# Retention and SwiGLU in one kernel: one step per chunk, subtractions of weight units on GpSimd, and a new layout of the first down stage

## The chip, the cores and the metric

The kernel runs on one core of a Trainium2 chip. The metric is the device time of one execution in microseconds (us), as a median over several runs. Engine names: PE is TensorE, DVE is VectorE, ACT is ScalarE, POOL is GpSimd, and SP is SyncE, whose queue issues most of the DMAs. Each engine takes its instructions strictly in the order of its own queue. Lines such as L707 are those of the kernel before.

## The reference, cut to what matters

```python
# q, k, v: (4, 8, 768, 64), float32; gamma and scale are constants of a head
for t in range(S):
    state = gamma * state + einsum('bhd,bhe->bhde', k[:, :, t], v[:, :, t])
    y[:, :, t] = scale * einsum('bhd,bhde->bhe', q[:, :, t], state)
x = y.transpose(0, 2, 1, 3).reshape(3072, 512)
g = x @ w_gate                        # 512 x 1536
h = g / (1 + exp(-g)) * (x @ w_val)   # w_val: 512 x 1536
return h @ w_out                      # 1536 x 512
```

## The kernel before, in words

The retention is computed in chunks of 128 time steps. For each chunk there are four pieces of work. `scores` multiplies k and q on PE (16 small matmuls, L385) and applies a decay mask on DVE (two operations, L391). `mix` forms the chunk's output y on PE from the old state (16 matmuls, L442; a sequence's first chunk has none) and from the masked scores (16 matmuls, L446), and ACT copies it to `xT` (L449). `state` brings the state up to date on PE (16 matmuls, L424) and DVE (L429), after ACT has decayed the old one (`decay`, four operations, L411). `scale_q` and `scale_k` scale operands on POOL (L399, L404).

The 3072 rows are worked on in four segments `s` of 2 x 384 rows (3 chunks of two sequences each). Each segment has an up stage (both of the first two weight matrices and the gate) and a down stage (the product with `w_out`). Both use a block scheme with seven products in place of eight, so sums and differences of blocks of the weights ("T" or "U" blocks) and of the activations are needed beforehand. The first segment's up stage is `up` (L513). The other three use `up2`, which applies the scheme a second time.

**The second up stages (`up2`).** They walk over 21 weight units `n`. A unit lies in one of six slots of `ring` and has seven products `U11, U1, U2, U22, U3, U21, U4`, of four matmuls each (L624), at the places `7n, 7n+2, ..., 7n+12` of an order that is sorted by these numbers, so that neighbouring units interleave. The products are added up in PSUM, and between them PSUM is read by ACT copies or DVE additions (both L589). For most units POOL adds two of these copies to older sums ("the diagonal", place `7n+2.6`, L589). A DVE addition at place `7n+8.5` needs that diagonal, and product `U4` at `7n+12` adds into the bank that this addition reads. POOL also forms sums for `hT` (L659), in two blocks, for two units of each seven. A whole unit (896 KB) is read back from DRAM (`unitt`) if its sums were formed earlier. Otherwise a 512 KB half (`unitb`) is read, three subtractions complete it (`sums_u`: one of 512 elements, L170, and two of 256, L178 and L174, in every partition), and a DMA of SP writes it to `unitt` for the later segments. A load of unit n+6 is issued at place `7n+13.2`.

**The down stages (`down`).** For each of three row blocks `u` there are seven products of 12 matmuls (L707, L716): `first` (into a bank that is copied), T1, T2, B22, T3, `second` and T4. The bank `x` is read by a DVE addition after T3 (L772) before T4 may add into it. After every product `step()` is called, 21 times in a stage, and carries a count `k`. In the first three down stages `step()` also hands out the retention of the next segment (the list `steps`), and in the down stage of segment 0 the loads and the subtractions of units 5, 7, ..., 19 and 0 to 3 as well (12 units, on DVE). What is left of the lists runs after the last product. Also in segment 0, the sums of the T blocks of `w_out` (`sums_d`, L289) and the states of the last two chunks of the first segment (`do("t4")`, `do("t5")`) lie between the first products. Activation sums for a row block are formed on DVE (`sum_h`, L695), and those for the next up stage by `sums_x` (L496 to L499) and `sums_2` (L578 to L581). After T4 ACT copies the last quarter (L778) and issues two DMAs to the output (L782).

In the first down stage no `second` stands between T3 and T4 for u = 0 and 1; in the others one does.

Of the kernel before, what the change touches and what calls it, by code (L numbers as in the profile page):

```python
# [16 lines left out]
P = 128  # L17
# [7 lines left out]
L = 3  # L25
# [8 lines left out]
RING = 6  # L34
# [7 lines left out]
def tile_retnet_swiglu(  # L42
# [79 lines left out]
    def seg_chunks(s):  # L122

        p, pos = divmod(s * L, NCK)
        return [(2 * p + i) * NCK + pos + j for j in range(L) for i in range(2)]
# [327 lines left out]
    def retention(s):  # L453

        cs = seg_chunks(s)

        def first(n):
            scores(cs[n])  # L460
            scale_k(cs[n])
            scale_q(cs[n])

        def last(n):
            decay(cs[n])
            state(cs[n])
            del chunks[cs[n]]
            if n + 3 < len(cs):
                load_chunk(cs[n + 3], places_of(n))

        steps = [lambda: first(0)]
        for n, c in enumerate(cs):
            if n + 1 < len(cs):
                steps.append(lambda n=n: first(n + 1))
            steps.append(lambda c=c: mix(c))
            steps.append(lambda n=n: last(n))
            if n % 2:
                steps.append(lambda n=n: sums_x(n // 2))
        return steps

# [102 lines left out]
    def up2(s, prepared, at_end):  # L583
# [4 lines left out]
        def at(t, fn, *args, **kw):  # L588
            events.append((t, len(events), lambda: fn(*args, **kw)))  # L589
# [17 lines left out]
        def stage(n):  # L607
# [61 lines left out]
                at(base + 13.2, load_unit, n + RING, n + RING in prepared)  # L669
            m = n + 2  # L670
            if m < NU and m not in prepared:
                for when, k in ((2.2, 0), (4.8, 1), (6.8, 2)):
                    at(base + when, lambda k=k: sums_u(m)[k]())

        for n in range(NU):
            stage(n)
# [23 lines left out]
    def down(s, u, step):  # L700
# [38 lines left out]
        if u == 0:  # L739
            first(0, range(2, FH))  # L740
            first(1)
            if s == 0:

                sums_d(0)
                sum_h(1, 0)
                second(0)
                do("t4")
                sum_h(2, 0)
                sums_d(1)
                second(1)  # L750
                do("t5")
                sum_h(4, 0)
                sum_h(3, 0)
                sums_d(2)
        elif u == 2:
            first(u)
        cur = dict(hs)
        wb = bank("wz")[:, :DH]
# [15 lines left out]
        step()  # L774
        if s or u == 2:
            second(u)
        product(x, T4, a_dn(1, 1, u), start=False)
        nc.scalar.copy(ev[1][:, :DH], x)  # L778
        p, pos = divmod(s * L, NCK)
        for i in range(2):  # L780
            row = (2 * p + i) * S + (pos + u) * P
            nc.scalar.dma_start(out=out[ds(row, P)], in_=ev[i])  # L782
        step()


    kept_vk = consts.tile([P, 2, 512], F32, name="kept_vk")
# [42 lines left out]
        g4 s5 S0 g5 x1 m4 a1 q5 C0 U T0 b1 m5 x2 U D D  # L829
    """)  # L830

    def retain(k):
        for _ in range(k):
            if steps:
                steps.pop(0)()

    for f in range(NF - 1):
        up(f)
# [9 lines left out]

    resident = list(range(RING - 2))
    to_sum = list(range(RING - 1, NU, 2)) + resident
    prepared = set(to_sum)

    for s in range(NSEG):
        nxt = seg_chunks(s + 1) if s + 1 < NSEG else []
        if s == 0:
            for i in range(3):
                load_chunk(nxt[i], places_of(i))
        else:  # L860

            ends = [(7 * n + 13.4, lambda i=i: load_chunk(nxt[i], places_of(i)))
                    for i, n in ((0, NU - 5), (2, NU - 4), (1, NU - 3)) if nxt]


            def begin(s=s):
                down(s, None, None)(0, range(2))

            ends.append((7 * (NU - 1) + 11, begin))
            for n in range(RING - 2, RING):  # L870
                ends.append((-1, lambda n=n: load_unit(n, n in prepared)))
            up2(s, prepared, ends)
            prepared = set(range(NU))
        if s:
            for n in (1, 2, 4, 3):
                sum_h(n, 0)
        steps = []
        if nxt:
            att.clear()
            steps = retention(s + 1) + [lambda ps=ps: sums_2(*ps)  # L880
                                        for ps in ((5, 6), (1, 2), (7,))]
        count, sums = [0, 0, 0], []

        def step():

            k = count[0] = count[0] + 1
            retain((k > 2) + (4 < k < 13) if s else (k > 5) + (7 < k < 18))
            if not nxt:
                return
            if s:  # L890
                if k > 7 and k % 2 == 0 and k // 2 - 4 < RING - 2:
                    load_unit(k // 2 - 4, True)
                return
            if count[1] < len(to_sum) and count[1] * 15 < (k - 5) * len(to_sum):
                n = to_sum[count[1]]
                load_unit(n, False, n if n in resident else count[1] % (RING - 2))
                sums.extend(sums_u(n))
                count[1] += 1
            while sums and count[2] * 15 < (k - 6) * 3 * len(to_sum):
                sums.pop(0)()  # L900
                count[2] += 1

        for u in range(L):
            down(s, u, step)
        for st in steps + sums:
            st()
        if nxt:
            sums_2(3)
            sums_2(4)

# [48 lines left out]
```

## Time and profile before

| | |
|---|---|
| median of 4 runs | 734.3 us (733.88 to 735.89) |
| profiled execution | 738.21 us, of which the span of the trace is 736.4 us |
| PE busy | 715.9 us (97% of the span) |
| DVE, ACT, POOL busy | 468.9, 239.6, 237.2 us |
| first up stage, to 146.7 us | first segment |
| first down stage, to 230.24 us | holds the retention of segment 1 and 12 units' subtractions |
| up2 of segment 1, from 230.24 to 331.78 us | 101.54 us |
| down of segment 1, to 407.77 us | 75.99 us |
| up2 of segment 2, to 505.28 us | 97.51 us |
| down of segment 2, to 581.96 us | 76.68 us |
| up2 of segment 3, to 679.14 us | 97.18 us |
| last down stage, to the end | no retention beside it |

How to read it: times count from the span's start, and a stage begins here with the start of its first matmul (the four to eight matmuls of the next stage that are drawn ahead are not counted apart). PE is "busy" from the start of a matmul to its modelled end, so matmuls that follow each other closely overlap and a busy PE may still run below its best pace; what a matmul really takes of the path is the distance from its start to the next one's start.

### The profile page before, as it was taken

How to read it: one execution, taken by the hardware profiler on the slowest of the kernel's cores; microseconds unless marked ns; L12 is line 12 of the kernel's file. 1: busy time of each engine (PE TensorE's matmuls, PEld its weight loads, DVE VectorE, ACT ScalarE, POOL GpSimd, SP SyncE). 2: the span in 40 equal slices, each digit the busy share in tenths (PEclk: the TensorE clock that was granted, in tenths of full speed). 3: DMA queues.
4: the chain of work that ended last, by engine and by line, in shares of the span. 5: the costliest groups of instructions: out<-in, count | busy, mean ns of one | idle time of the engine just before them, and what ended most of it. 6: DMA issues, size and time to landing. Idle time of an engine off the chain costs nothing.

```text
span 736.4 us, 11713 instructions
## 1 busy us (share of the span) xinstructions
PE 715.9 (97%) x4544; PEld 618.0 (84%) x4544; DVE 468.9 (64%) x836; ACT 239.6 (33%) x484; POOL 237.2 (32%) x147
## 2 busy tenths in 40 slices
PE   7998999999999999999999999999999999999997
PEld 6754555577878999998888999998888999999886
DVE  3687998777668788886454465757526356667420
ACT  2558777511122333321121324332121133233000
POOL 0423444503200638280310174464210063726000
PEclk9899999999999999999999999999999999999999
DMA  8698887703998867671643355560283055540010
GB/s 309 211 350 277 273 289 255 278 1 104 406 347 308 298 219 265 236 240 33 210 162 126 128 201 201 200 215 20 87 301 131 28 200 201 200 150 1 1 57 29
DMA packets 60824, 139.06 MB, mean 189 GB/s; under 512 B 4576, under 2 KB 27616, under 8 KB 60768
## 3 DMA queue, kind: packets, MB, share of 16 engines
q1 hardware_dynamic: 57312, 132.01, 51.7%
q10 hardware_dynamic: 3456, 6.29, 2.3%
q8 instruction: 36, 0.59, 0.3%
q14 instruction: 20, 0.16, 0.1%
HBM read 101.72 MB, written 36.57 MB: 188 GB/s over the span
## 4 chain that ended last, share of the span: by engine, by line
PE 87%; DVE 4%; issue 1%; ACT 1%; DMA 1%; ACTq 0%; SPq 0%; DVEq 0%
PE bank L624 38%; PE bank L707 23%; PE bank L513 14%; PE bank L716 4%; PE bank L385 3%; PE bank L446 2%; PE bank L442 2%; PE bank L424 1%; DMA ring<-unitb 1%; DVE iop L589 0%; DVE ring L289 0%; DVE ring L170 0%; DVE midp L391 0%; ACT midp L589 0%; DVE hsp L695 0%
## 5 line engine op out<-in xcount | busy, mean ns | idle before, releaser
L624 PE MATMUL bank<-loadp,ring 128*128 128x192 f32 x720 | 140.7, 327 | 3.1 <-ACT midp L589 2.5
L707 PE MATMUL bank<-wot,hsp 128*128 128x256 f32 x576 | 131.7, 383 | 0.0
L624 PEld LDWEIGHTS bank<-loadp,ring 128*128 128x128 f32 x720 | 120.5, 190 | 4.8 <-ACT midp L589 3.6
L707 PEld LDWEIGHTS bank<-wot,hsp 128*128 128x128 f32 x576 | 107.5, 190 | 16.6 <-issue 1.0
L589 DVE TENSOR_TENSOR iop<-bank,iop 128x384 f32<-128x384 f32 x144 | 79.7, 555 | 56.2 <-PE bank L624 53.2
L624 PE MATMUL bank<-xs,ring 128*128 128x192 f32 x432 | 87.9, 326 | 0.0
L659 POOL TENSOR_TENSOR hT<-iop 128x768 f32<-128x768 f32 x36 | 66.4, 1845 | 36.8 <-DVE iop L589 36.8
L589 ACT COPY hsp<-bank 128x384 f32<-128x384 f32 x90 | 42.8, 478 | 100.5 <-PE bank L624 89.8
L589 POOL TENSOR_TENSOR iop<-hsp,midp 128x768 f32<-128x768 f32 x9 | 16.3, 1813 | 181.6 <-ACT hsp L589 181.6
L624 PEld LDWEIGHTS bank<-xs,ring 128*128 128x128 f32 x432 | 73.2, 190 | 0.0
L707 PE MATMUL bank<-wot,hT 128*128 128x256 f32 x288 | 66.2, 383 | 2.5 <-DVE iop L772 2.5
L513 PE MATMUL bank<-xs,ring 128*128 128x384 f32 x192 | 64.7, 488 | 3.2 <-DVE xs L496 1.8
L624 PE MATMUL bank<-xT,ring 128*128 128x192 f32 x324 | 66.2, 327 | 1.1 <-DVE iop L589 1.1
L707 PEld LDWEIGHTS bank<-wot,hT 128*128 128x128 f32 x288 | 53.8, 190 | 10.8 <-DVE iop L772 2.8
L513 PEld LDWEIGHTS bank<-xs,ring 128*128 128x128 f32 x192 | 36.1, 190 | 30.0 <-issue 2.4
L624 PE MATMUL bank<-hsp,ring 128*128 128x192 f32 x288 | 56.8, 327 | 0.0
L624 PEld LDWEIGHTS bank<-xT,ring 128*128 128x128 f32 x324 | 54.8, 190 | 2.3 <-DVE iop L589 2.2
L589 DVE TENSOR_TENSOR midp<-bank,midp 128x384 f32<-128x384 f32 x72 | 40.0, 555 | 22.8 <-PE bank L624 21.2
L513 PE MATMUL bank<-xT,ring 128*128 128x384 f32 x144 | 49.3, 488 | 1.6 <-DVE hT L550 1.6
L624 PEld LDWEIGHTS bank<-hsp,ring 128*128 128x128 f32 x288 | 48.4, 190 | 0.5 <-ACT hsp L589 0.5
L449 ACT COPY xT<-bank 128x512 f32<-128x512 f32 x24 | 14.1, 586 | 95.1 <-PE bank L446 95.0
L513 PEld LDWEIGHTS bank<-xT,ring 128*128 128x128 f32 x144 | 27.1, 190 | 21.0 <-DVE hT L550 2.2
(146 smaller groups left out, 971.0 us busy)
## 6 DMA issues: line engine op xcount, KB each, us to landing
ring<-unitt SPq DMA_DIRECT2D x50, 896.0 KB, 4.6
unitt<-ring SPq DMA_DIRECT2D x21, 896.0 KB, 4.7
unitb<-ring SPq DMA_DIRECT2D x12, 896.0 KB, 7.4
ring<-unitb SPq DMA_DIRECT2D x21, 512.0 KB, 6.5
out_dram<-iop ACTq DMA_DIRECT2D x24, 256.0 KB, 3.5
loadp<-in_w_val_dram SPq DMA_DIRECT2D x18, 256.0 KB, 3.9
loadp<-in_w_gate_dram SPq DMA_DIRECT2D x9, 512.0 KB, 6.6
midp<-in_w_out_dram SPq DMA_DIRECT2D x12, 256.0 KB, 6.3
```

Source lines behind the costliest of these rows:

```text
L385: nc.tensor.matmul(sp[i][:, ts(n, P)], kt[r, n], qt[r, n], start=True, stop=True, skip_group_check=True)
L424: nc.tensor.matmul(st[ds(D * i, D), n], kd[:, h], vn[:, h], start=(n == 0), stop=True, skip_group_check=True)
L442: nc.tensor.matmul(y[r, ts(n, P)], prev[r, n], qd[r, n], start=(n == 0), stop=False, skip_group_check=True)
L446: nc.tensor.matmul(y[ds(D * i, D), ts(n, P)], vn[:, ts(2 * n + i, D)], a[i][:, n], start=(ci == 0 and n == 0), stop=True, skip_group_check ...
L449: nc.scalar.copy(xT[:, :, c // NCK % 2, ts(ci % L, P)], pairs(y))
L513: nc.tensor.matmul(o, w[:, slot, k], a[:, k], start=(start and k == 0), stop=(stop and k == KH - 1), skip_group_check=True)
L589: events.append((t, len(events), lambda: fn(*args, **kw)))
L624: nc.tensor.matmul(o[:, h], w[:, h, slot], rhs, start=(start and h == 0), stop=True, skip_group_check=True)
L659: by_block(9.5, 13.5, lambda r: pool(to[:, r], u2[:, r], p5[:, r], op=add))
L707: nc.tensor.matmul(o, a[:, k], wot[k][:, slot], start=(start and k == 0), stop=(k == FH - 1), skip_group_check=True)
L716: nc.tensor.matmul(o, a_dn(0, 0, u)[:, k], wot[k][:, B11], start=(k == 0), stop=(k == FH - 1), skip_group_check=True)
```

## The change

Five edits, all in the order of the work; no arithmetic is added or left out.

1. `retention` makes one step of each chunk: scores of chunk n+1, then mix, decay and state of chunk n and the load of chunk n+3, then the two scalings of chunk n+1. Before, these were three steps, with products of the down stage between them. The steps are handed out at fixed counts, `DUE`, where before `retain` took one or two at a time.
2. `sums_2(1, 2)` moves to right after the last chunk's step, `sums_2(5, 6)` is the last step, and `sums_2(7)` runs after the last product.
3. In the first down stage the states of both last chunks are put together, and for u = 0 and 1 a product stands between T3 and T4: `second(1)` and `first(2)`, which were elsewhere in the same stage.
4. In the first three down stages the last row block's output DMAs are issued at place 5 of the following up2 and not at the end of the down stage.
5. The first down stage prepares 10 units (5, 7, ..., 19, 0, 1) and no longer 12. It loads units 2 and 3 too, but their three subtractions, as those of 4, 6, ..., 20, are done by POOL in the up2 of segment 1 (11 units there; before 9, on DVE), at places 4.1 to 4.3 and not 2.2 to 6.8. Loads of units begin after the second product of the first down stage, three ahead of the subtractions.

```diff
 def retention(s):
-        def first(n):
-            scores(cs[n])
-            scale_k(cs[n])
-            scale_q(cs[n])
-        def last(n):
-            decay(cs[n])
-            state(cs[n])
-            del chunks[cs[n]]
-            if n + 3 < len(cs):
-                load_chunk(cs[n + 3], places_of(n))
-        steps = [lambda: first(0)]
-        for n, c in enumerate(cs):
+        def chunk(n):
             if n + 1 < len(cs):
-                steps.append(lambda n=n: first(n + 1))
-            steps.append(lambda c=c: mix(c))
-            steps.append(lambda n=n: last(n))
-            if n % 2:
+                scores(cs[n + 1])
+            if n >= 0:
+                mix(cs[n])
+                decay(cs[n])
+                state(cs[n])
+                del chunks[cs[n]]
+                if n + 3 < len(cs):
+                    load_chunk(cs[n + 3], places_of(n))
+            if n + 1 < len(cs):
+                scale_k(cs[n + 1])
+                scale_q(cs[n + 1])
+        steps = []
+        for n in range(-1, len(cs)):
+            steps.append(lambda n=n: chunk(n))
+            if n == 5:
+                steps.append(lambda: sums_2(1, 2))
+            if n > 0 and n % 2:
                 steps.append(lambda n=n: sums_x(n // 2))
...
 # up2, stage n
-                for when, k in ((2.2, 0), (4.8, 1), (6.8, 2)):
-                    at(base + when, lambda k=k: sums_u(m)[k]())
+                for when, k in ((4.1, 0), (4.2, 1), (4.3, 2)):
+                    at(base + when, lambda k=k: sums_u(m, nc.gpsimd)[k]())
...
 # down, u == 0 and s == 0
-                do("t4")
+                do("t4 t5")
                 sum_h(2, 0)
                 sums_d(1)
-                second(1)
-                do("t5")
...
-        elif u == 2:
+        elif u == 2 and s:
             first(u)
...
         if s or u == 2:
             second(u)
+        else:
+            (second, first)[u](u + 1)
         product(x, T4, a_dn(1, 1, u), start=False)
         nc.scalar.copy(ev[1][:, :DH], x)
-        for i in range(2):
-            row = (2 * p + i) * S + (pos + u) * P
-            nc.scalar.dma_start(out=out[ds(row, P)], in_=ev[i])
+        def store():
+            for i in range(2):
+                row = (2 * p + i) * S + (pos + u) * P
+                nc.scalar.dma_start(out=out[ds(row, P)], in_=ev[i])
+        if u < L - 1 or s == NSEG - 1:
+            store()
         step()
+        return store
...
+    DUE = [(5, 7, 9, 10, 11, 13, 14, 15, 17, 18, 19, 20),
+           (3, 5, 7, 8, 9, 11, 12, 13, 15, 16, 18, 20)]
...
-    resident = list(range(RING - 2))
+    resident = [0, 1]
...
+            ends.append((5, store))
             up2(s, prepared, ends)
...
-            steps = retention(s + 1) + [lambda ps=ps: sums_2(*ps)
-                                        for ps in ((5, 6), (1, 2), (7,))]
+            steps = retention(s + 1) + [lambda: sums_2(5, 6)]
 def step():
-            retain((k > 2) + (4 < k < 13) if s else (k > 5) + (7 < k < 18))
...
             if s:
+                if k in DUE[1]:
+                    steps.pop(0)()
...
-            if count[1] < len(to_sum) and count[1] * 15 < (k - 5) * len(to_sum):
-                n = to_sum[count[1]]
-                load_unit(n, False, n if n in resident else count[1] % (RING - 2))
-                sums.extend(sums_u(n))
+            if count[1] < len(to_sum) + 1 and k > 1 and count[1] < 3 + count[2] // 3:
+                n = (to_sum + [2])[count[1]]
+                load_unit(n, False, count[1] % (RING - 2))
+                if n in prepared:
+                    sums.extend(sums_u(n))
                 count[1] += 1
-            while sums and count[2] * 15 < (k - 6) * 3 * len(to_sum):
+            if k in DUE[0]:
+                steps.pop(0)()
+            while sums and count[2] * 12.5 < (k - 6) * 3 * len(to_sum):
...
         for u in range(L):
-            down(s, u, step)
-        for st in steps + sums:
+            store = down(s, u, step)
+        for st in sums:
             st()
+        if s == 0:
+            load_unit(3, False)
         if nxt:
+            sums_2(7)
             sums_2(3)
             sums_2(4)
```

## The prediction

> **What bounds the kernel.** I read the page first.
>
> ```profile
> PE 715.9 (97%) x4544; PEld 618.0 (84%) x4544; DVE 468.9 (64%) x836; ACT 239.6 (33%) x484; POOL 237.2 (32%) x147
> PE 87%; DVE 4%; issue 1%; ACT 1%; DMA 1%; ACTq 0%; SPq 0%; DVEq 0%
> ```
>
> PE is the bound, busy 97% of the span and 87% of the chain that ended last. The change takes no matmul away, so a gain can only come from matmuls that start closer together. Next, the chain in order of time (start, length, what), in the down stage of segment 2 and in the last one, which has no retention:
>
> ```profile
> 513.44 2.79 PE bank L707 x12
> 516.23 1.09 PE bank L385 x16
> 517.32 2.79 PE bank L707 x12
> 520.11 1.02 PE bank L442 x16
> 521.13 1.02 PE bank L446 x16
> 522.15 0.46 PE bank L424 x16
> ...
> 531.33 0.62 PE bank L424 x16
> ...
> 683.46 31.08 PE bank L707 x144
> ```
>
> Undisturbed, a product of 12 takes 31.08/12 = 2.59 us. Between small matmuls it takes 2.79. So each interruption costs 0.20 us beyond its own matmuls. A state (L424) right behind its own mix takes 0.46, alone 0.62.
>
> Then who made PE wait (us in total, times, longest):
>
> ```profile
> PE bank L707 <- DVE iop L772: 2.5, 2, 1.8
> PE bank L624 <- ACT midp L589: 2.5, 4, 1.3
> PE bank L624 <- DVE iop L589: 1.8, 3, 0.7
> ```
>
> The timeline gives their places. Since a matmul's end is modelled, I measure a stall from start to start:
>
> ```profile
> 175.37 0.63 PE L424 MATMUL bank<-loadp 128*64 128x64 f32 x16
> 177.77 0.92 PE L707 MATMUL bank<-wot,hT 128*128 128x256 f32 x3 [1.77 <-DVE iop L772]
> ...
> 230.89 0.81 PE L624 MATMUL bank<-loadp,ring 128*128 128x192 f32 x4
> 232.45 1.57 PE L624 MATMUL bank<-loadp,ring 128*128 128x192 f32 x8 [0.75 <-ACT midp L589]
> ```
>
> The first pair is T4 in the first down stage, which waits for a DVE read (2.40 us from start to start, 0.56 without the wait). The second is the start of an up2 (1.56, where four matmuls take 0.65). Last, the three up2 stages side by side (length, then busy time of PE, PEld, DVE, ACT, POOL, clock, DMA share, GB/s). The first is 4.0 us longer and its DVE has 22 us more to do:
>
> ```profile
> 230.24:331.78 101.54, 98.08 (x594) 96.01 (x592) 81.58 (x142) 33.84 (x66) 54.10 (x30) 1.00 0.73 262
> 407.77:505.28 97.51, 96.95 (x594) 96.20 (x592) 59.47 (x104) 34.12 (x66) 49.48 (x28) 1.00 0.52 180
> ```
>
> **The change part by part.**
>
> **One step per chunk.** In the timelines of the three down stages with retention I count 13, 12 and 11 places where small matmuls stand between products. In the order of the changed program there are 8, 7 and 7 (seven steps, and t4 with t5). That is 14 fewer at 0.20: 2.8 us. Seven states stood apart from their mix (2, 3 and 2) and now follow it, at 0.62 - 0.46 = 0.16: 1.1 us. Together 3.9 us, on the path. The new waits inside a step have cover. Mix n needs masks and scaled q of scores n, which ran a chunk step earlier. Between the two chunk steps lie two products (5.4 us), the rest of that step (2.5) and scores n+1 (1.1), 9 us against 1.4 for two masks (0.68 each) and 2.4 for the POOL scalings (1.31 and 1.11). On DVE the state addition now waits about 1.2 us for matmuls with the rest of the queue behind it; DVE is busy 61.9 of the 85.2 us from 146.7 to 231.92, so up to 6 us of that fit. I take 0; without the cover each of 20 steps could hold PE, and at 0.1 us each that is 2 us.
>
> **A product between T3 and T4.** The two stalls on L772 are 2.40 - 0.56 = 1.84 and (202.25 to 203.64) 1.39 - 0.56 = 0.83, together 2.7 us. The read was late because DVE was behind by activation sums slowed beside POOL (1.90 and 1.68 us for the pair where one alone is 0.95), masks and unit subtractions. Now 2.6 us of a product lie between, which covers both. What is late next is T4 of u = 2, where sums_2(1, 2) (4 x 0.55) and two subtractions stand before L772 in DVE's queue: 0.42 + 2.2 + 0.9 + 0.4 = 3.9 us after B22 ends, against two products, 5.2. It holds by 1.3. First use of the T blocks comes 2.8 us earlier, since `second(1)` left its place: sums_d(1) would end at about 160.3 (its row ends there now), and T2 would start at 160.0 and need its last block 2.2 us later. It holds.
>
> **The late output DMAs.** They stood in ACT's queue before the first copy of up2. PE lost 1.56 - 0.65 = 0.91 us there, and at 408.91 and 583.09 0.36 each, 1.6 in all. At place 5 they stand between copies at 4.5 and 7.5, two products (1.3 us) apart, and an issue takes 0.34 to 1.16. They read space that up2 first writes at place 16.6, near 10 us; issued at 3.2 us with a landing of 2.1 to 8.3, they are most often done. I take a gain of 1.6, and 0 to 0.7 lost.
>
> **Subtractions on POOL.** Removed are two PE stalls in the first up2, both behind subtractions: 0.85 at 243.4 (a 512 subtraction that ran 1.81) and 1.48 at 264.8 (L174 ahead of L663, for which an ACT copy waited). 2.3 us.
>
> What POOL pays the trace shows only by neighbours: 1.27 for 512 elements (L399) and 1.81 for 768, so 0.73 for 256 on that line, and 2.73 for a unit. Two multiples bound a 256: 0.64 from below, 1.27 from above (as long as a 512), so 2.6 to 3.8 a unit. I take 2.73, from the nearest shapes. 11 units are 30 us on 49, 79 of 97. The stage has room, its middle less. These rows are from the second up2, where POOL runs as it will there:
>
> ```profile
> 453.99 1.81 POOL L659 TENSOR_TENSOR hT<-iop 128x768 f32<-128x768 f32 x1 [2.13 <-DVE iop L589]
> ...
> 463.09 1.81 POOL L659 TENSOR_TENSOR hT<-iop 128x768 f32<-128x768 f32 x1 [1.84 <-DVE iop L589]
> 464.86 1.81 POOL L589 TENSOR_TENSOR hT<-hsp,hT 128x768 f32<-128x768 f32 x1
> 466.63 1.82 POOL L659 TENSOR_TENSOR hT<-iop 128x768 f32<-128x768 f32 x1
> 468.53 1.81 POOL L589 TENSOR_TENSOR iop<-hsp,iop 128x768 f32<-128x768 f32 x1
> ```
>
> In this seven (units 7 to 13) unit 12's subtractions fall before the row at 463.09, whose 1.84 us of idle time swallow all but 0.9; unit 14's stand before 466.63 and add 2.73. So unit 13's diagonal (468.53) ends not at 470.34 but at 474.0, and its DVE addition at 474.6. U4 of unit 13 is due after 100 products of 0.65 from 407.77 + 0.36, at 473.3: PE waits 1.3 us. The same for units 0 to 6 and 14 to 20 gives 0.1 each. I add 0.6 where L663 meets a POOL operation (0.95 alone, 1.3 to 1.8 beside one), and 0.5 at the start, where subtractions of units 2 and 3 on POOL meet sums_2(3) and (4). New waits: 2.6 us, net loss 0.3. Bounds: no new wait (a gain of 2.3) and every POOL operation 20% slower, as rows of 2.19 beside DVE's own subtractions show (a loss near 13, the last rival). SP's queue: the store of unit n+2 now stands before the load of unit n+5 and holds it until POOL is done, at most 4 us late; that unit is used 18 us later, and loads landed in 6.8 (9.7 at worst). 0.
>
> The Trainium skill, GPSIMD Engine Reference, section 4.1, speaks against this edit: it gives elementwise work on a tile to VectorE, as GpSimd is about half as fast on two inputs. Its figure, 4497 ns for 2048 elements, would make a unit about 2.2 us of stream time, an estimate, and the wait at unit 13 some 0.9 shorter. The rows here agree on the ratio (0.69 on DVE, 1.27 on POOL) but not on the verdict, since in this stage DVE is the engine that PE waits for.
>
> Two units fewer take 3.9 us from DVE in the first down stage, off the path. Loads begin earlier there, in a stretch (150 to 175) where DMA stood near 0. 0.
>
> **Sum.** 3.9 + 2.7 + 1.6 - 0.3 = 7.9 us less. The profiled execution, 738.2, would become 730.3, its span 728.5. It lies 3.9 above the median of 734.3; the same difference on the median gives 726.4.
>
> **Rivals.**
> - All cover holds and POOL never delays PE: 3.9 + 2.7 + 1.6 + 2.3 = 10.5, so 723.8. For it: POOL idles half of the stage. Against: the 0.9 us at unit 13 that are missing by the bare count. Chance 0.2.
> - DVE stays behind in the first down stage, since each step's state addition now blocks it, and the stalls at T4 come back at another product, or the steps cost 0.1 to 0.2 each: the 2.7 goes and 1 more with it, 730.1. For it: DVE has 9.80 of 10 us from 170 to 180. Chance 0.14.
> - No change: the counted interruptions cost nothing when merged, because PE meets new waits of their size. The order of the changed program shows fewer places, so the edit does what it says, and only waits could undo it. 734. Chance 0.03.
> - Slower: POOL becomes the bound of the first up2. If its 768 operations take 2.19 and a unit 3.3, the middle seven have 9 x 2.19 + 2 x 3.3 = 26.3 us between two diagonals that PE passes in 22.8. That is 3.5 too many, and with DVE and the next load waiting behind I take 5 for each of three sevens, 15 in all. 10.5 - 15 gives 4.5 us more, 738.8. It decides once a unit costs POOL over 4 us: the waits 0.1, 1.3 and 0.1 grow by two units a seven, and 1.5 + 6 x (4.05 - 2.73) = 9.4 eats what the edits leave (10.5 less 0.6 and 0.5). Against: the rows of 2.19 stood beside DVE's subtractions, which are gone; without them they are 1.81. Chance 0.08.
>
> My forecast has 0.55, from 724.5 to 728.5. The range takes in the first rival and the second with 1.4 us for the unknown costs: 722.8 to 731.5. A measurement of this kernel can tell about 0.2% from no change, 1.5 us. Faster 0.88, same 0.04, slower 0.08.
>
> **What would show it.** In the changed profile the three down stages should hold products of 2.79 only at 8, 7 and 7 places. No PE wait on L772's successor should be left in the first down stage. The gap before the third product of each up2 should fall under 0.1 us. The first up2 should be about 98.5 to 101 us, L589 on DVE untouched, and a PE wait should appear near its unit 13. Wrong would be a first up2 over 103 us, POOL without idle time there, or new PE waits inside the steps.

## The result and the profile after

The changed kernel takes 736.1 us (median of 31 runs, 733.27 to 739.65), the kernel before 734.01 on the same chips (50 runs, 733.27 to 737.27). The ratio is 1.0027, with a 95% interval of 1.0019 to 1.0036: slower by a small margin, where the prediction had 726.4 and 722.8 to 731.5. Lines below are those of the kernel they belong to; in the changed one many stand two further down (L624 became L626, L707 became L709), while L772 kept its number.

The page of the changed kernel: busy times of the engines, then the chain that ended last, by engine.

```profile
PE 710.9 (97%) x4544; PEld 616.5 (84%) x4544; DVE 455.1 (62%) x803; ACT 239.8 (33%) x484; POOL 270.1 (37%) x180
...
PE 81%; POOL 7%; DVE 3%; issue 2%; DMA 1%; ACT 1%; POOLq 0%; DVEq 0%; ACTq 0%
```

POOL was not in the chain before; now it has 7%. The chain in order of time, in the down stage of segment 2, shows the part that came as forecast: two products in a row (5.38 for 24 matmuls, twice 2.69), then scores, mix and state as one block, and the states shown at 0.46.

```profile
509.82 5.38 PE bank L709 x24
515.19 1.09 PE bank L385 x16
516.28 1.02 PE bank L442 x16
517.31 1.02 PE bank L446 x16
518.33 0.46 PE bank L424 x16
518.79 5.38 PE bank L709 x24
```

What made PE wait (us in total, times, longest) shows the other part:

```profile
PE bank L626 <- ACT midp L591: 2.8, 4, 1.1
PE bank L626 <- DVE iop L591: 2.3, 5, 0.7
...
PE bank L626 <- DVE midp L591: 1.4, 2, 0.8
PE bank L709 <- DVE hsp L697: 1.1, 1, 1.1
...
PE bank L626 <- DVE hT L591: 0.7, 1, 0.7
```

The two waits on L772 (2.5 us) are gone, but the up2 has more than before. The first up2 by windows (length, busy PE, PEld, DVE, ACT, POOL, clock, DMA share, GB/s):

```profile
221.88:328.40 106.52, 99.68 (x593) 95.72 (x592) 67.18 (x118) 33.98 (x66) 80.82 (x58) 1.00 0.72 256
```

DVE has 14 us less to do than before, POOL 27 more, and the stage is 5 us longer. By stages, from first to last matmul of a stage (and a down stage from the last matmul of one stage to the first of the next), in us:

| stage | before | after | difference | forecast by the terms of the sum |
|---|---|---|---|---|
| first down | 81.86 | 78.54 | -3.3 | -4.0 |
| up2 of segment 1 | 101.38 | 106.51 | +5.1 | -0.6 |
| down of segment 1 | 76.16 | 76.01 | -0.15 | -1.5 |
| up2 of segment 2 | 97.35 | 97.09 | -0.26 | -0.36 |
| down of segment 2 | 76.84 | 75.75 | -1.09 | -1.1 |
| up2 of segment 3, last down | 150.32 | 150.06 | -0.26 | -0.36 |
| sum | 583.91 | 583.96 | +0.05 | -7.9 |

So in the traces everything that was won is lost again in the first up2 and just behind it. The medians differ by 2 us more, and there the granted clock (the share of its full clock that TensorE gets) differs from run to run. The profile of before has a stretch at about half of it, at 16.9 to 23.8 us (clock in the third column from the right):

```profile
17.00:24.00 7.00, 5.88 (x56) 5.36 (x58) 2.79 (x6) 0.58 (x4) 2.27 (x2) 0.52 1.07 367
```

In the profile of the changed kernel, its fastest run, the same window has 1.00. Over all runs it is the other way round: 17 of the changed kernel's 31 have a mean granted clock under 0.999 (their median is 737.5, that of the others 734.9), and 15 of 98 runs of the kernel before beside the experiments below (735.9, the others 733.8). Where in the changed kernel's other runs the half clock falls, no profile shows. Where profiles of other kernels have it, it lies at 17 to 31 us, but in two it lies in a traced stage: b_steps has it at 175.1 to 178.5 us and a_place at 292.9 to 296.3. Times below go with the traced stages, and these two are marked.

### The profile page after: what moved, and what is told of

The parts are those of the page before. It is cut to its first block, busy times and chain, and to the rows that moved or that the text cites. A ratio compares the mean times of both kernels' runs of the same rounds, so it can differ in the third digit from the quotient of the medians.

```text
span 731.5 us, 11752 instructions
## 1 busy us (share of the span) xinstructions
PE 710.9 (97%) x4544; PEld 616.5 (84%) x4544; DVE 455.1 (62%) x803; ACT 239.8 (33%) x484; POOL 270.1 (37%) x180
## 4 chain that ended last, share of the span: by engine, by line
PE 81%; POOL 7%; DVE 3%; issue 2%; DMA 1%; ACT 1%; POOLq 0%; DVEq 0%; ACTq 0%
PE bank L626 29%; PE bank L709 26%; PE bank L515 14%; PE bank L718 3%; PE bank L385 3%; PE bank L446 3%; PE bank L442 2%; POOL hT L661 2%; POOL iop L591 2%; DMA out_dram<-iop 1%; PE bank L424 1%; POOL ring L170 1%; POOL hT L591 1%; DVE hT L665 1%; DVE iop L591 1%
## 5 line engine op out<-in xcount | busy, mean ns | idle before, releaser
L626 PE MATMUL bank<-loadp,ring 128*128 128x192 f32 x720 | 140.7, 327 | 3.0 <-ACT midp L591 2.8
L709 PE MATMUL bank<-wot,hsp 128*128 128x256 f32 x576 | 129.8, 382 | 1.1 <-DVE hsp L697 1.1
L626 PEld LDWEIGHTS bank<-loadp,ring 128*128 128x128 f32 x720 | 120.4, 190 | 5.2 <-ACT midp L591 3.3
L709 PEld LDWEIGHTS bank<-wot,hsp 128*128 128x128 f32 x576 | 108.0, 190 | 17.1 <-DVE hsp L697 1.5
L591 DVE TENSOR_TENSOR iop<-bank,iop 128x384 f32<-128x384 f32 x144 | 79.6, 556 | 67.1 <-PE bank L626 58.4
L626 PE MATMUL bank<-xs,ring 128*128 128x192 f32 x432 | 88.2, 327 | 1.2 <-DVE hT L591 0.7
L591 ACT COPY hsp<-bank 128x384 f32<-128x384 f32 x90 | 43.0, 478 | 102.7 <-PE bank L626 92.7
L661 POOL TENSOR_TENSOR hT<-iop 128x768 f32<-128x768 f32 x36 | 65.4, 1815 | 26.9 <-DVE iop L591 26.9
L626 PEld LDWEIGHTS bank<-xs,ring 128*128 128x128 f32 x432 | 73.0, 190 | 2.1 <-DVE hT L591 1.3
L626 PE MATMUL bank<-xT,ring 128*128 128x192 f32 x324 | 66.5, 328 | 3.0 <-DVE iop L591 1.7
L709 PE MATMUL bank<-wot,hT 128*128 128x256 f32 x288 | 65.5, 381 | 0.0
L591 POOL TENSOR_TENSOR iop<-hsp,midp 128x768 f32<-128x768 f32 x9 | 16.3, 1814 | 128.8 <-ACT hsp L591 124.7
L709 PEld LDWEIGHTS bank<-wot,hT 128*128 128x128 f32 x288 | 54.3, 190 | 7.6 <-issue 0.2
L626 PEld LDWEIGHTS bank<-xT,ring 128*128 128x128 f32 x324 | 54.7, 190 | 5.2 <-DVE iop L591 3.1
L626 PE MATMUL bank<-hsp,ring 128*128 128x192 f32 x288 | 56.6, 326 | 0.0
L591 DVE TENSOR_TENSOR midp<-bank,midp 128x384 f32<-128x384 f32 x72 | 39.8, 556 | 19.6 <-PE bank L626 13.8
L626 PEld LDWEIGHTS bank<-hsp,ring 128*128 128x128 f32 x288 | 48.5, 190 | 0.0
L768 DVE TENSOR_TENSOR iop<-bank,iop 128x256 f32<-128x256 f32 x12 | 5.1, 425 | 67.3 <-PE bank L709 50.3
```

The costliest lines, as they stand in the source:

```text
L626: nc.tensor.matmul(o[:, h], w[:, h, slot], rhs, start=(start and h == 0), stop=True, skip_group_check=True)
L661: by_block(9.5, 13.5, lambda r: pool(to[:, r], u2[:, r], p5[:, r], op=add))
L709: nc.tensor.matmul(o, a[:, k], wot[k][:, slot], start=(start and k == 0), stop=(k == FH - 1), skip_group_check=True)
```

## The experiments

A theory from these traces: the subtractions on POOL cost all of it, by POOL's queue and because two-input operations of POOL and DVE hold each other up. The rivals were the late output DMAs, the places of the subtractions, and the merged steps.

**The engine of the subtractions, and the late output DMAs.** Four kernels: the changed one with the subtractions on DVE at the old places; with the output DMAs of segment 0 back at the end of the down stage; with both; and unchanged.

```diff
 # a_dve
-                for when, k in ((4.1, 0), (4.2, 1), (4.3, 2)):
-                    at(base + when, lambda k=k: sums_u(m, nc.gpsimd)[k]())
+                for when, k in ((2.2, 0), (4.8, 1), (6.8, 2)):
+                    at(base + when, lambda k=k: sums_u(m)[k]())
 # a_store
-        if u < L - 1 or s == NSEG - 1:
+        if u < L - 1 or s in (0, NSEG - 1):
             store()
...
-            ends.append((5, store))
+            if s > 1:
+                ends.append((5, store))
 # a_both: both; a_same: neither
```

> The changed kernel, with the subtractions of the first up2 back on DVE at places 2.2, 4.8 and 6.8 (11 units, all else as changed). Theory A (POOL's queue is what holds PE in the first up2): that stage falls from 106.5 us to 100 to 102, the late diagonals at units 5, 12 and 13 go, the 1.28 us wait at the start of the next down stage goes too, and the median falls by about 6 us, to 728 to 730. Theory B (the late output DMAs hold the stage, since the sums at place 16.6 write where the DMAs still read): DVE's first writes to that space wait as POOL's do, the stage stays at 104 us or more, and the median falls by 2 us at most. Theory C (nothing in this stage, the change costs elsewhere): no change.

> The changed kernel, with the last output DMAs of the first down stage issued at its end, as before (in the other two down stages they stay late). Theory A: POOL starts its first diagonal some 4 us earlier but is still the bound of the middle seven units; the first up2 falls by 1 to 2 us to about 105, the median to 734.5 to 735.5. Theory B: the first up2 falls to about 102, and the spread from run to run (733.3 to 739.7) shrinks to about 1.5 us, since it is the landing of these DMAs that varies; median 731 to 732. Theory C: no change or a loss of the 0.9 us at the stage's start.

> The changed kernel with both: subtractions of the first up2 on DVE at the old places, and the first segment's output DMAs at the end of the down stage. Theory A: as with the subtractions alone, within 1 us. Theory B: as with the DMAs alone, within 1 us, or both together are needed: first up2 at 101 to 102 us and a median of 728 to 729. If the first up2 stays over 104 in all three, both fall.

> The changed kernel once more, unaltered, beside the others on the same chip. It shows the spread of its spans and granted clocks from run to run. Theory A and B: 736 with a spread of several us, the spread being in the first up2. Theory C: the spread is in the first 40 us of the span, where the profile before had a granted clock of 0.77 to 0.91, and belongs to the start.

Measured, with the ratio to before: 727.68 for a_dve (0.9911, 0.9898 to 0.9923), 733.75 for a_store (0.9998, 0.9986 to 1.0009), 726.52 for a_both (0.9907, 0.989 to 0.9925), 735.63 for a_same (1.0026, 1.001 to 1.0041). Putting the subtractions back on DVE, at their old places, wins 8 us, and makes a kernel that beats the one before by 0.9%. Its first up2 by windows:

```profile
224.22:324.46 100.24, 97.88 (x592) 95.81 (x591) 83.14 (x148) 33.77 (x66) 53.91 (x30) 1.00 0.75 270
```

That is 6.3 us shorter than in the changed kernel, and 1.3 more come at the next stage's first product. The late output DMAs cost 2.0 us of the first up2 (104.51 without them), but only in company with POOL's subtractions: a_both's stage has the 100.25 of a_dve. In the changed kernel POOL's first diagonal overwrites what they read, and waited for them (idle time and releaser in brackets):

```profile
235.04 1.81 POOL L591 TENSOR_TENSOR iop<-hsp,midp 128x768 f32<-128x768 f32 x1 [4.07 <-DMA out_dram<-iop]
236.81 1.27 POOL L170 TENSOR_TENSOR ring<-ring 128x512 f32<-128x512 f32 x1
```

**The same edits made alone on the kernel before.** b_pool is before with the subtractions of its nine units on POOL at the new places; b_steps with the merged steps, their fixed counts and the moved `sums_2`; b_prod with the product between T3 and T4 and t4 with t5; b_store with the late output DMAs.

```diff
 # b_prod
-                do("t4")
+                do("t4 t5")
                 sum_h(2, 0)
                 sums_d(1)
-                second(1)
-                do("t5")
...
-        elif u == 2:
+        elif u == 2 and s:
             first(u)
...
         if s or u == 2:
             second(u)
+        else:
+            (second, first)[u](u + 1)
         product(x, T4, a_dn(1, 1, u), start=False)
```

> The kernel before, with nothing but its 9 unit subtractions of the first up2 moved to POOL, at places 4.1 to 4.3. Theory A (POOL's in-order queue with two units a seven holds PE, whatever the rest): the first up2 grows from 101.4 us to 104 to 107, the next down stage by 1.3, the median by 4 to 7 us, to 738 to 741. Theory B (POOL is late only because the first diagonal waits for the late output DMAs): no growth beyond 1 us, 734 to 735. Theory D (POOL takes over where DVE was late, as forecast): 0 to 2 us faster.

> The kernel before, with nothing but one step per chunk and its counts (with the moved sums_2). The forecast's working: interruptions of the products fall from 13, 12 and 11 to 8 (t4 and t5 stay apart, so 9), 7 and 7, 0.20 us each and 0.16 for each state behind its mix: 3.5 to 4 us less, 730 to 731; the two waits for L772's successor in the first down stage stay within 1 us of their 2.7. Rival (the steps bring waits of their own inside them): 733 or more, with new waits at small matmuls in the down stages.

> The kernel before with two edits of the first down stage alone: the product between T3 and T4, and t4 with t5. The prediction has 2.7 us for the stalls at T3 and T4 and 0.2 for one interruption less; the wait of 0.76 between t4 and t5 that the changed kernel showed comes off: first down stage 81.86 less 2.1 = 79.7 us, time 2.1 us shorter than before, 732. If the cover was only lent (DVE late at another product, since steps are not merged here and DVE has two units more to subtract), the stage stays over 81.5 us and the time within 0.7 us of before.

> The kernel before with the late output DMAs alone. By the prediction 1.6 us less (0.9 at the first up2, 0.36 at each other), 732.7. By the traces of the changed kernel 0.26 in segments 2 and 3 and the 0.9 in the first, 1.4 in all, if nobody waits for the landing; if POOL's first diagonal waits for it as it did with the subtractions on POOL (4 us), the first up2 gets no shorter than 100.5 + 1 and the whole is 0.5 less or nothing.

b_pool took 741.96 (1.0095, 1.0076 to 1.0115). Its first up2 is 104.17 against 101.38, although DVE's own two waits there (0.85 and 1.48) are gone, and its next stage begins 1.2 us late. In all its traced stages are 4.1 us longer than those of before; the rest of the 7.7 us by which its median is longer lies outside them (all of its five runs have a mean clock under 0.999, and its profile has the half clock at 18 to 22 us). So the subtractions lose without any of the other edits too, by 4.1 us.

b_steps took 733.19 (0.9975, 0.9961 to 0.9989) and b_prod 735.42 (1.0016, 1.0003 to 1.003). Neither does alone what was expected: their first down stages last 83.00 and 82.12 us, against 81.86 before and 78.54 in the changed kernel. Of b_steps' 83.00 about 1.7 is the half clock, in the first row below: 12 matmuls take 4.54 us there and 2.86 in the second. With merged steps alone the reads after T3 stay late (lines there are one further than before, L773 is L772):

```profile
174.46 4.54 PE L708 MATMUL bank<-wot,hT 128*128 128x256 f32 x12 [2.10 <-DVE iop L773]
...
201.34 2.86 PE L708 MATMUL bank<-wot,hT 128*128 128x256 f32 x12 [0.78 <-DVE iop L773]
```

With the product alone they are gone, but now scores wait, for the masks (L391) that stand in DVE's queue behind three activation sums:

```profile
166.89 1.75 PE L385 MATMUL bank<-loadp 64*128 64x128 f32 x16 [1.83 <-DVE midp L391]
```

In the changed kernel both waits are gone. A reading that fits is that the two edits need each other: the product covers T4, and the fixed counts of the merged steps keep masks away from the backlog. It is not shown, as no kernel here has these two alone: the changed one also prepares two units fewer in this stage (6 subtractions on DVE) and loads units earlier. In the other two down stages b_steps wins what the changed kernel should have (74.70 and 75.75 us, against 76.16 and 76.84). But its first up2 grew from 101.38 to 102.76, by a wait of 2.10 us for an addition on DVE that stands behind activation sums, the moved ones among them:

```profile
236.86 0.92 PE L625 MATMUL bank<-xT,ring 128*128 128x192 f32 x4 [2.10 <-DVE midp L590]
```

b_store took 734.28 (1.0003, 0.9988 to 1.0017). Its traced stages are 0.9 us shorter than those of before: 0.27 in each of segments 2 and 3, 0.4 in the first up2. There the gap of 0.9 us at the start is gone, and the wait behind the 512 subtraction grew from 0.85 to 1.23, since that subtraction now waits 1.64 us for its load, where it waited 1.20.

**Which units.** a_mid puts units 12 and 14, the two around unit 13, back on DVE; a_best leaves only units 2 and 3 on POOL and moves unit 8's subtractions, on DVE, behind its L665. a_best2 is the same kernel again: the profiled execution of a_best took 4209 us, with PE busy 100% of it (4202 us, before 716), for no reason that its trace shows, so its trace can't be read for waits.

```diff
 # a_best
-                for when, k in ((4.1, 0), (4.2, 1), (4.3, 2)):
-                    at(base + when, lambda k=k: sums_u(m, nc.gpsimd)[k]())
+                on_pool = m in (2, 3)
+                whens = (4.1, 4.2, 4.3) if on_pool else (9.0, 9.1, 9.2) if m == 8 else (2.2, 4.8, 6.8)
+                engine = nc.gpsimd if on_pool else nc.vector
+                for k, when in enumerate(whens):
+                    at(base + when, lambda k=k: sums_u(m, engine)[k]())
 # a_mid
+                on_dve = m in (12, 14)
+                whens = (2.2, 4.8, 6.8) if on_dve else (4.1, 4.2, 4.3)
+                engine = nc.vector if on_dve else nc.gpsimd
```

> The changed kernel, with units 12 and 14 back on DVE at the old places, so that POOL has none of its subtractions in the middle seven units. Theory A: the waits of that seven (0.61, 1.21, 0.85 and 1.26 us) go and with them the 3.5 us between matmuls 392 and 490 of the stage; what the first and last seven cost stays; 735.6 falls to 731 to 732.5. Rival (what costs is the total of POOL's work or its sharing of SBUF with DVE, spread over the stage): a fall in proportion, 2 of 11 units, 1.5 us.

> The changed kernel, with the subtractions of units 4 to 20 back on DVE, those of unit 8 at places 9.0 to 9.2 of their stage, behind both products of h0 with p1 (L665 there), and those of units 2 and 3 left on POOL, which idles then. Theory A: against all 11 on DVE the 1.47 us wait before unit 7's second product goes (there L174 stood ahead of L665, for which an ACT copy waits), and the 0.52 at the stage's start; the first up2 takes 98.3 to 99 us and the median is 725.5 to 726.5. Rival (the three subtractions in one place hold DVE's queue longer than they save): 727.5 to 729.

> The kernel of a_best once more, for its trace: subtractions on POOL for units 2 and 3 only, those of unit 8 on DVE late in the unit, all others on DVE as before. Of the three waits that a_dve kept in the first up2 (0.52 at the start, 1.47 at unit 8, 0.86 near the end) the first two should go: 100.24 - 2.0 = 98.3 us, and the time 2 us under a_dve, 725.7. If the late subtraction only moves the wait to another place, the stage stays at 100 us and the time at 727.7.

a_mid took 732.67 (0.9972, 0.996 to 0.9984): two units of eleven give back 3.1 us of the stage (103.44), between units 10 and 17. a_best took 728.3 (0.9909, 0.9891 to 0.9927) and a_best2 726.81 (0.9912, 0.989 to 0.9935). The stage of a_best2 is 100.65 us, so the wait at unit 8 went and others of 0.6, 0.6, 0.3 and 0.7 us came: as good as a_dve, no better.

**The places.** On POOL the subtractions stand at 4.1 to 4.3, on DVE they stood at 2.2, 4.8 and 6.8. a_place is the changed kernel with them on DVE at the new places, a_pplace with them on POOL at the old ones (the line of a_dve above, with the one or the other half of its edit).

> The changed kernel with the subtractions back on DVE, but at the three places of the changed kernel (4.1, 4.2, 4.3, behind each other) and not at 2.2, 4.8 and 6.8. If the engine is what costs (POOL's queue, and the two engines stretching each other), the first up2 stays near the 100.2 us of a_dve, at most 102 since three subtractions in a row (2.3 us) sit in front of L590's additions, and the time is 727.5 to 730. If the place is what costs, the stage keeps at least 104 us and the time is 732 or more.

> The changed kernel with its subtractions on POOL, but at 2.2, 4.8 and 6.8 of a unit as in the kernel before, and not at 4.1 to 4.3 behind the diagonal. On DVE the places decided 13.7 us of the first up2 (113.9 against 100.2). If places matter as much on POOL, the stage falls from 106.5 to 102 or less and the time to 731.5 or less. If on POOL only the sum of its work counts, since nobody but its own queue stands behind a subtraction there, the stage stays at 105 to 108 us and the time at 734.5 to 737.5; the first subtraction then stands ahead of the diagonal, so rather longer than shorter.

a_place took 739.7 (1.008, 1.0063 to 1.0098), a_pplace 731.95 (0.9975, 0.9958 to 0.9991). The first up2, in us:

| | at 2.2, 4.8, 6.8 | at 4.1, 4.2, 4.3 |
|---|---|---|
| on DVE | 100.24 | 113.92 |
| on POOL | 103.04 | 106.51 |

About 1.7 of the 113.92 is a_place's half clock. Both count, and the places more than the theory had it, which put DVE at the new places at 102 us at most. At 4.1 the 512 subtraction meets POOL's diagonal, in a_place so:

```profile
256.29 1.81 POOL L591 TENSOR_TENSOR iop<-hsp,iop 128x768 f32<-128x768 f32 x1
```

and on DVE, where the three block the additions that PE waits for:

```profile
256.47 2.19 DVE L170 TENSOR_TENSOR ring<-ring 128x512 f32<-128x512 f32 x1
258.69 0.42 DVE L178 TENSOR_TENSOR ring<-ring 128x256 f32<-128x256 f32 x1
259.15 0.43 DVE L174 TENSOR_TENSOR ring<-ring 128x256 f32<-128x256 f32 x1
259.49 0.55 DVE L591 TENSOR_TENSOR iop<-bank,iop 128x384 f32<-128x384 f32 x1
```

**What about POOL costs.** Two kernels keep the changed kernel's places, but POOL fills the tiles and reads nothing: they leave the differences out, so only their time counts. a_light fills each tile once, a_queue two or three times.

```diff
-                for when, k in ((4.1, 0), (4.2, 1), (4.3, 2)):
-                    at(base + when, lambda k=k: sums_u(m, nc.gpsimd)[k]())
+                for slot, times in zip((slice(U1, U3 + 1, 3), U2, U4), (3, 2, 2)):   # a_light: (1, 1, 1)
+                    for _ in range(times):
+                        at(base + 4.1, lambda slot=slot: nc.gpsimd.memset(units[m][:, :, slot], 0.0))
+                at(base + 4.3, lambda: nc.sync.dma_start(out=unit_t[m], in_=units[m]))
```

> The changed kernel with each subtraction of the first up2 replaced by a fill of the same tile on POOL (the difference is left out): one input fewer than none, about 1.1 us of POOL a unit where the subtractions take 2.73. First up2 without subtractions on either engine would be 98 us. Both theories: 98 to 100 us.

> As the kernel with fills, with each fill done two or three times, so that POOL is held for about as long as by the subtractions (2.5 to 3 us a unit) but reads nothing. If POOL's time in its queue is what the subtractions cost, the first up2 has the 106 us of the changed kernel, 104 at least. If it is the reading, POOL's and DVE's two inputs beside each other, it has 101 us or less, and the multiplications on L665 take 0.95 again.

a_light took 725.45 (0.9889, 0.9875 to 0.9903), a_queue 733.64 (0.9997, 0.9988 to 1.0006). In a_queue a fill of 512 took 0.526 us and one of 256 0.312, so a unit holds POOL for 3 x 0.526 + 4 x 0.312 = 2.83 us, about what the subtractions take (1.42 + 0.91 + 0.73 = 3.06, the means in the changed kernel's stage). The first up2 of a_queue:

```profile
222.29:328.48 106.19, 99.15 (x593) 95.74 (x592) 64.58 (x115) 34.03 (x66) 77.20 (x98) 1.00 0.72 254
```

106.19 against 106.52 with subtractions, and against 98.76 in a_light, where a unit holds POOL for 1.15 us. The next stage's first product waits 1.25 us in a_queue too, and 0.39 in a_light. That the first two are so close is in part luck: the stage has one wait for the landing of the late output DMAs (PE waits for a DVE addition, and that for the DMA), and it is longer in a_queue. First the changed kernel, then a_queue with the DVE addition:

```profile
235.62 1.57 PE L626 MATMUL bank<-loadp,ring 128*128 128x192 f32 x8 [0.20 <-DVE iop L591]
236.59 1.57 PE L626 MATMUL bank<-loadp,ring 128*128 128x192 f32 x8 [1.55 <-DVE iop L591]
235.98 0.56 DVE L591 TENSOR_TENSOR iop<-bank,midp 128x384 f32<-128x384 f32 x1 [2.95 <-DMA out_dram<-iop]
```

Counted from that product on, the stage lasts 92.8 us in the changed kernel and in a_same, 91.9 in a_queue and 85.0 in a_light. So of the 7.8 us between a_light and the changed kernel the time for which POOL is held costs 6.9, and what is left for the subtractions' reading (and for the 0.2 us by which a unit of fills is shorter) is 0.9. The half of the theory with the reading falls as the main cause, not wholly. What it says of POOL and DVE holding each other up still plays its part through the operations that POOL had before: in a_queue too the first L665 of the middle seven takes 2.39 us, beside POOL's L661 (290.10 to 291.91) and the diagonal behind it:

```profile
290.33 2.39 DVE L665 TENSOR_TENSOR hT<-hT,midp 128x768 f32<-128x768 f32 x1
```

**A copy of the kernel before.**

> The kernel before, unchanged, under a name of its own. The changed kernel has a traced span of 731.5 against 731.0 to 732 for before at a full clock, yet a median 2.1 us longer, since more of its runs show a clock of 0.998 or less from their first 30 us. If that belongs to the kernel, this copy has the median of before (733.7 to 734.3). If it belongs to how the runs are taken, it comes out 1 to 2 us above it, 735 to 736, and the changed kernel is then the same as before rather than slower.

b_same took 733.84, before 733.72 beside it (1.0003, 0.9994 to 1.0013), and only 2 of its 11 runs had a mean clock under 0.999. In a_same 6 of 12 had one, with 735.63 against 733.96 for before beside it. So the 2 us beyond the stages belong to the changed kernel and not to how its runs were taken. How the change brings the half clock about more often no run here shows; it stays open.

## Why the prediction failed, step by step

**Subtractions on POOL: the step that failed.** The prediction took a net loss of 0.3 us: 2.3 removed, 2.6 of new waits. Traced, the step costs 6.3 us in the first up2 and 1.3 behind it, 7.6 against the same kernel with DVE. Its inputs were right: a unit took 1.27 + 0.73 + 0.73 us where nothing stood beside it, and POOL is busy 80.8 of 106.5 us, where 30 on 49, 79 of 97, were worked out. The wrong part was how a busy POOL becomes time: the forecast asked only when a diagonal ends and which product follows it, and found one place, unit 13 (1.3 us). The changed kernel's timelines show three more in the same seven. POOL from 288.85:

```profile
288.85 0.73 POOL L174 TENSOR_TENSOR ring<-ring 128x256 f32<-128x256 f32 x1
289.54 1.80 POOL L661 TENSOR_TENSOR hT<-iop 128x768 f32<-128x768 f32 x1
291.42 2.40 POOL L591 TENSOR_TENSOR iop<-hsp,iop 128x768 f32<-128x768 f32 x1
293.79 1.26 POOL L170 TENSOR_TENSOR ring<-ring 128x512 f32<-128x512 f32 x1
```

DVE beside it:

```profile
289.82 2.34 DVE L665 TENSOR_TENSOR hT<-hT,midp 128x768 f32<-128x768 f32 x1
293.86 0.56 DVE L591 TENSOR_TENSOR iop<-bank,iop 128x384 f32<-128x384 f32 x1 [1.70 <-POOL iop L591]
294.33 1.53 DVE L665 TENSOR_TENSOR hT<-hT,midp 128x768 f32<-128x768 f32 x1
```

and PE:

```profile
292.89 0.89 PE L626 MATMUL bank<-loadp,ring 128*128 128x192 f32 x4 [1.05 <-ACT midp L591]
294.47 0.92 PE L626 MATMUL bank<-xT,ring 128*128 128x192 f32 x4 [0.69 <-DVE iop L591]
296.48 0.76 PE L626 MATMUL bank<-loadp,ring 128*128 128x192 f32 x3 [1.09 <-ACT midp L591]
```

The subtractions push POOL's operation of L661 beside the multiplication L665, which takes 2.34 us in place of 0.95; an ACT copy needs its result, and PE the copy (1.2 us lost). The diagonal behind it ends at 293.8, so the DVE addition sits idle for 1.70 us (PE 0.85, the wait at unit 13 that was forecast at 1.3), and the second L665 stands behind that addition in DVE's queue and so meets the next subtraction (PE 1.26). With 0.6 just before, at 282.5, for a diagonal that DVE waited 2.43 us for, this seven loses 3.9 us where 1.3 was forecast. The 0.6 for L663 meeting POOL was in the sum, but once for the whole stage. In the first seven the subtractions of units 2 and 3 and the wait for the output DMAs come on top; 0.5 was set for that.

The rival that POOL slows the first up2 (738.8, chance 0.08) was right in kind, but not its condition. It was to decide from 4 us a unit, with POOL the bound. At 2.7 to 3.1 us, with POOL idle a quarter of the time, it decided already. Of the signs that the prediction named for being wrong, the first up2 over 103 us came, and POOL without idle time did not. Nor was the bare count of DVE's relief worth anything: DVE's 14 us less could take away no more than the 2.3 that had been waits. And the places, which the prediction did not price apart, make 3.5 us of it on POOL.

**One step per chunk: right.** 8, 7 and 7 interruptions were left. In segment 2 the stage became 1.09 us shorter, by the working 4 x 0.20 + 2 x 0.16 = 1.1. In segment 1 it is 1.45 with subtractions on DVE (5 x 0.20 + 3 x 0.16 = 1.5); in the changed kernel the wait of 1.3 us at the first product hides it.

**A product between T3 and T4: the cover held, one wait was missed.** Both stalls are gone. But the first down stage fell by 3.3 and not 4.0, as the states t4 and t5 now stand behind each other: 1.26 us from start to start, 0.7 more than the 0.56 of a state with a product behind it. The second starts just after the DVE addition of the first (L429) has ended, at 152.38, which fits a bank that both use; the profile itself names no releaser.

```profile
152.48 0.69 PE L424 MATMUL bank<-ring,ring 128*64 128x64 f32 x16 [0.57 <-issue]
```

The rival with DVE late at another product (730.1, chance 0.14) is what b_prod shows: with steps not merged, and two units more to subtract.

**Late output DMAs: 0.26 each where 0.36 was taken, and a wrong landing.** "Most often done" was not so in the first up2: the second of them landed after 10.1 us, where the sum had 2.1 to 8.3, and POOL and DVE waited for it (4.07 and 1.60 us). With POOL's subtractions that cost 2.0 us. The 0.91 at the start of this stage went as forecast, but other waits took most or all of it back: b_store's stage is 0.4 shorter, and with the subtractions on DVE the stage lasts the same without them (a_both 100.25) as with them (a_dve 100.24).

Without the POOL step the rest of the sum was 8.2 us; a_dve's stages are 7.5 shorter than those of before (576.38 against 583.91), which is the 8.2 less the 0.7 of t4 and t5. In the first up2 that agreement is luck: a_dve is 1.1 us shorter there than before, but so is a_both, whose output DMAs are not late.

## What to carry to other kernels

Moving work to an idle engine is not priced by its busy share: list what that engine delivers, and for each delivery who waits, and what stands behind the waiting instruction in *its* queue, since a late addition here delayed a multiplication that made the next copy late. Try the place before the engine: three subtractions spread between other operations cost less on either engine than the same three in a row behind the diagonal. And when two edits act on the same queue, run each alone: here neither gained more than half a microsecond in the first down stage by itself (b_steps' half clock taken off), and both together, with two units fewer to prepare, gained 3.3 us. Then run the pair alone too, which was not done here.

## What the runs showed of the hardware

A DVE operation with two SBUF inputs does not just run slowly beside one of POOL; by these rows it waits it out. In a_pplace, POOL from 288.48:

```profile
288.48 1.82 POOL L591 TENSOR_TENSOR iop<-hsp,iop 128x768 f32<-128x768 f32 x1
290.24 1.27 POOL L170 TENSOR_TENSOR ring<-ring 128x512 f32<-128x512 f32 x1
291.59 1.32 POOL L178 TENSOR_TENSOR ring<-ring 128x256 f32<-128x256 f32 x1
```

and DVE:

```profile
288.82 3.51 DVE L665 TENSOR_TENSOR hT<-hT,midp 128x768 f32<-128x768 f32 x1
```

The multiplication is issued at 288.82, POOL is free of the first two at 291.5, and 0.8 us later L665 ends (292.3); then POOL's next one, 0.73 elsewhere, took 1.32, which fits a wait in its turn. The additions of L591 on DVE, with one input in PSUM, keep their 0.54 to 0.56 throughout. Beside fills, which read nothing, no such wait shows: in a_queue the second L665 of the same seven stands beside fills (294.32 to 297.2) and takes its usual time, where the changed kernel's took 1.53 beside a subtraction.

```profile
294.89 0.95 DVE L665 TENSOR_TENSOR hT<-hT,midp 128x768 f32<-128x768 f32 x1
```

The half clock lasted 3.4 us where it came in a traced stage, and in both cases began just behind a gap on PE: 0.6 us after one of 2.10 us in b_steps, 0.3 us after one of 2.13 in a_place. But b_steps' other gap of 2.10 us, at 236.86, was not followed by one, so what decides it stays open.

The Trainium skill (SBUF — State Buffer, "Who interferes with whom") states the same: a DVE instruction with two SBUF inputs contends with a GpSimd instruction that reads SBUF and not with one that only writes it; it calls the shared ports an exclusive lock, and says that issue order decides who blocks. The prediction priced this as a stretch of 0.6 us in all; a row for each meeting of the two engines would have come nearer. The skill's rule that the prediction set aside (GPSIMD Engine Reference, section 4.1, "Engine selection") gave the right verdict at the old places (100.24 us on DVE, 103.04 on POOL): two-input work on a tile belongs on VectorE. At the new places DVE was the worse engine (113.92 against 106.51), so where in the queue the work stands counted as much as the engine.
